# The work beside a recurrence gathered into one clump per slot

## The chip, the cores and the metric

The kernel runs on one core of one Trainium2 chip. The number that counts is the device time of one execution in microseconds; the kernel before takes 2278.77 us, the median of 3 runs (2270.02 to 2282.51). The core's engines run side by side, each through its own queue in order: PE (TensorE, with the weight load shown as PEld), DVE (VectorE), ACT (ScalarE), POOL (GpSimd) and SP, which issues the DMAs. They wait for each other through semaphores.

## The reference

Three layers follow each other. The first is a delta-rule recurrence over 768 tokens, for 4 batches of 8 heads of 48; the second a soft mixture of 8 experts over all 3072 tokens; the third a plain two-layer net.

```
for t in range(S):                                   # attention
    y[:, :, t] = einsum('bhd,bhde->bhe', q[:, :, t], state)
    v_old = einsum('bhde,bhd->bhe', state, kt)
    state = state + bt * einsum('bhd,bhe->bhde', kt, vt - v_old)
P = exp(logits - logits.max());  8 x (rows, then columns normalised)
out += P[:, e:e + 1] * (relu(x @ w1[e]) @ w2[e])     # for every expert e
h = x @ w_in;  h * sigmoid(1.702 h) @ w_out          # last layer
```

## The kernel before

The recurrence is done in 24 blocks of 64 tokens, one after the other (`u` = 0 to 23), each for two batches and all heads. `Attention.chain(u)` is the part that must be in order. It has four steps, `s` = 0 to 3, and each ends in one group of small fp32 matmuls and what frees them: `ks` (state times keys; DVE then makes `r`), `up` (the triangular inverse `tt` times `r`; ACT copies it to `su`), `sp` (the state's update; DVE makes `S`), `y` (the output; ACT makes `ys`). The stretch of the program that one step and all the work beside it take is a slot, and the slots are numbered 4u + s.

Beside the chain, three other kinds of work are put into the slots.

- `Attention.prep(g)` prepares the next group of four blocks; g counts the groups. It is a generator, and each `yield` is a piece. Its order is fixed: eight Gram pieces (`gram`, tile `pg`: 8 small matmuls, then three DVE products `am`, `x`, `x`), two ACT copies of `am`, a DVE transpose to `ln`, thirty steps of a triangular inverse on DVE alone (each an `lt` and an `ln` product, half a piece each), a transpose to `ta`, and then `pz`, `pz`, `px`, `px` (32 small matmuls each, copied by ACT) with DVE's transpose to `tt` and two ACT copies among them. How many pieces a slot gets is in `PIECES` (`FIRST` for the first 16 slots).
- `expert0(n)` is the first expert on the pair of blocks n, in full-array matmuls: `ph` (three matmuls of 256 columns per item; after three items ACT and DVE make the two halves of `h`) and `po` (three matmuls of 384 columns per item). One call of `expert_item` emits one item. Some five items fall on a slot (`ITEMS`, `RATE`), from slot 10 on.
- Once per block, at s = 1, `emit_x` turns the block before: PE transposes `ys` into `xt`, ACT and DVE split it into the two halves of `xb`, ACT copies it once more, and SP stores it. At even `u` the pair is then complete, its gates `pl` (9 matmuls on `xb`) come at s = 2, and their transpose `pt` at s = 3. The pair's `ph` read `xb` too.

The tiles `pg`, `pz`, `px`, `xt`, `pl` and `pt` share two PSUM buffers (pool `psg`): the third of them waits until the first has been read. `ph` has two buffers of its own. What the experts' items do not do beside the recurrence is done right after it by the same function; there is a fixed number of items in all (480).

In `slot` of the kernel before, the items are spread: a share before each piece and one after the last. `xt`, `pl` and `pt` are emitted ahead of the slot's pieces, and `xt` has at least one item in front of it.

Of the kernel before, what the change touches and what calls it, by code (L numbers as in the profile page):

```python
# [34 lines left out]
LAG = 10  # L35
# [5 lines left out]
class Attention:  # L41
# [127 lines left out]
    def gram(self, u, planes, h0, n, pool=None):  # L169


        nc, x, j, bm = self.nc, self.X[u // 2 % 4], u % 2, self.bm.get(u)
        hs = slice(h0, h0 + n)
        where, tag = pool or (self.psg, "g")
        ps = where.tile([128, n, len(planes), 64], F32, tag=tag, name="pg")
        for h in range(n):
            for b in range(2):
                dr = slice(64 * b, 64 * b + D)
                nc.tensor.matmul(  # L179
                    ps[64 * (1 - b):64 * (1 - b) + 64, h], x[dr, 0, j, h0 + h],  # L180
                    x[dr, planes[0] * (1 + b):planes[-1] * (1 + b) + 1:1 + b, j, h0 + h], start=True, stop=True)
        m = 8 * (u % 4) + h0
        if planes[0] == 0:
            nc.vector.tensor_tensor(out=self.am[:, m:m + n], in0=ps[:, :, 0], in1=bm[:, hs], op=ALU.mult)
        if planes[-1] == 1:
            for b in range(2):
                p = slice(64 * (1 - b), 64 * (1 - b) + 64)
                m = x[p, 1 + b, j, hs]
                if u < 4:
                    nc.scalar.copy(out=m, in_=ps[p, :, len(planes) - 1])  # L190
                else:
                    nc.vector.tensor_tensor(out=m, in0=ps[p, :, len(planes) - 1], in1=bm[p, hs], op=ALU.mult)
# [7 lines left out]
    def prep(self, g):  # L200

        nc, am, tt = self.nc, self.am, self.tt
        w, u = 2 * g, 4 * g
        if g == 0:
            self.square(0, nc.vector)
            self.square(1, nc.vector)
            self.norm(0)
            self.norm(1)
            self.weigh(0, 1)
            self.mask(0, eng=nc.vector)  # L210
            for v in range(1, 4):
                self.mask(v)
            for v in range(4):
                self.gram(v, (0,), 0, H, (self.psc, "c") if v < 2 else None)
            self.scale_v(0)
            self.scale_k(0)
            self.scale_k(1)
            self.square(2)
            yield 1.0
        else:  # L220
            for i in range(8):
                if i == 5:
                    self.mask(u + 3)
                self.gram(u + i // 2, (0, 1), i % 2 * 4, 4)
                if i == 1:
                    self.square(w + 1)
                elif i == 2:
                    self.norm(w + 1)
                elif i == 3:
                    self.weigh(w + 1)  # L230
                    self.mask(u + 2)
                elif i == 7:
                    self.scale_k(w)
                    self.scale_k(w + 1)
                yield 1.0

        ln = self.one.tile([128, 32, 32], F32, tag="ln", name="ln")

        for q in (32, 96):
            nc.scalar.copy(out=am[q:q + 32, :, 0:32], in_=am[q:q + 32, :, 32:64])  # L240
            yield 1.0
        nc.vector.transpose(out=ln, in_=am[:, :, 0:32].rearrange("p m t -> p t m"))
        yield 1.0
        nc.vector.memset(ln.rearrange("p t s -> p (t s)")[:, 0:1024:33], 1.0)
        for jj in range(1, 31):
            tmp = self.one.tile([128, 256], F32, tag="lt", name="lt")
            nr = 31 - jj
            t3 = tmp[:, 0:nr * jj].rearrange("p (a c) -> p a c", c=jj)
            nc.vector.tensor_tensor(  # L249
                out=t3, in0=ln[:, jj + 1:32, jj:jj + 1].to_broadcast([128, nr, jj]),  # L250
                in1=ln[:, jj:jj + 1, 0:jj].to_broadcast([128, nr, jj]), op=ALU.mult)
            yield 0.5
            nc.vector.tensor_tensor(out=ln[:, jj + 1:32, 0:jj], in0=ln[:, jj + 1:32, 0:jj], in1=t3, op=ALU.add)  # L253
            if g == 0 and jj < 5:
                self.gram(jj - 1, (1,), 0, H)

            if g < NG - 1:
                if jj == 17 and g > 0:
                    self.square(w + 2)
                elif jj == 21:  # L260
                    self.norm(w + 2)
                elif jj == 22:
                    step = self.weights(w + 2)
                elif jj > 22:
                    next(step, None)
            if jj == 30 and g < NG - 1:
                for v in range(2):
                    if g == 0:
                        self.mask_m(v)
                for v in range(2):  # L270
                    self.mask(u + 4 + v)
                    if g == 0:
                        self.mask_m(2 + v)
            yield 0.5
        ta = self.one.tile([128, 32, 32], F32, tag="ta", name="ta")
        nc.vector.transpose(out=ta.rearrange("p m s -> p s m"), in_=ln.rearrange("p t s -> p s t"))
        yield 1.0

        zs = ta

        def pz(m0, n):
            ps = self.psg.tile([128, n, 32], F32, tag="g", name="pz")
            for m in range(n):
                for q in (0, 64):
                    nc.tensor.matmul(ps[q + 32:q + 64, m], am[q:q + 32, m0 + m, 32:64],
                                     ta[q:q + 32, m0 + m], start=True, stop=True, tile_position=(q, q + 32))
            for q in (0, 64):
                nc.scalar.copy(out=zs[q + 32:q + 64, m0:m0 + n], in_=ps[q + 32:q + 64])

        def px(m0, n):  # L290
            ps = self.psg.tile([128, n, 32], F32, tag="g", name="px")
            for m in range(n):
                for q in (0, 64):
                    nc.tensor.matmul(ps[q:q + 32, m], zs[q + 32:q + 64, m0 + m],
                                     tt[q + 32:q + 64, m0 + m, 32:64], start=True, stop=True,
                                     tile_position=(q + 32, q))
            for q in (0, 64):
                nc.scalar.copy(out=tt[q:q + 32, m0:m0 + n, 32:64], in_=ps[q:q + 32])

        def tr(q):  # L300
            if q is None:
                nc.vector.transpose(out=tt[:, :, 32:64].rearrange("p m t -> p t m"), in_=ln)
            else:
                nc.scalar.copy(out=tt[q:q + 32, :, 0:32], in_=tt[q:q + 32, :, 32:64])

        for f, *i in (((pz, 0, 16), (tr, None), (pz, 16, 16), (tr, 0), (tr, 64), (px, 0, 16), (px, 16, 16)) if g else
                      ((pz, 0, 8), (tr, None), (tr, 0), (tr, 64), (px, 0, 8), (pz, 8, 8), (px, 8, 8),
                       (pz, 16, 16), (px, 16, 16))):
            while f == tr and self.upped < u - 1:
                yield 1.0  # L310
            f(*i)
            if f == px and i[0] == 0:
                self.ready = g
            yield 1.0
# [105 lines left out]
def kernel(  # L420
# [47 lines left out]
    A = Attention(tc, actx, ident, X, kq, kw, vw, bu, psg)  # L468
# [201 lines left out]
    ex = []  # L670
# [21 lines left out]
        while done < due and expert_item():  # L692
            done += 1

    def slot(t):

        n, k = rate * ITEMS[t % 16] if t >= LAG else 0, (PIECES if t > 15 else FIRST)[t % 16]
        if t == LAG:
            expert(BURST)
        i = 0  # L700
        while i < k:
            expert(n / (k + 1) * step[0])
            step[0] = next(prep, 1.0)
            i += step[0]
        expert(n / (k + 1))

    step = [1.0]
    build = sums(0, 0)
    for u in range(NU):
        for s, _ in enumerate(A.chain(u)):  # L710
            if s == 1 and u > 0:
                if 4 * u >= LAG:
                    due -= 1
                    expert(1)
                    done += expert_item()
                while u % 2 == 1 and len(ex) > 1:
                    done += expert_item()
                emit_x(u - 1, A.xt())
                if u % 2 == 0:
                    ex.append(expert0(u // 2 - 1))  # L720
            if s > 1 and u > 0 and u % 2 == 0:
                (logits if s == 2 else turn)(u // 2 - 1)
            slot(4 * u + s)
            while A.ready < u // 4:
                next(prep)
            next(ew, None)
            if u > 12:
                next(build, None)
# [418 lines left out]
```

## Time and profile before

| | |
|---|---|
| median of 3 runs | 2278.77 us (2270.02 to 2282.51) |
| the profiled execution | 2276.9 us, of which the span is 2275.2 us |
| PE busy in the span | 2169.0 us |
| DVE busy in the span | 1515.7 us |
| mean granted clock of TensorE, 1.00 being full | 0.982 |

In a row of the timeline, PE's shape is that of the stored weight (rows by columns), then that of the output. An fp32 matmul is recorded as two, so a Gram piece of 8 matmuls stands as x16 and a piece of `px` as x64. PE's durations contain the way through the array, so one matmul's end lies after the next one's start; what a matmul costs in a stream is the distance between starts. "L458" to "L460" are the three matmuls of `mm3`, which every full-array product is made of.

### The profile page before, as it was taken

What the parts mean: (1) busy time and instruction counts of PE and PEld (TensorE: products, weight loads), DVE (VectorE), ACT (ScalarE), POOL (GpSimd) and SP (SyncE); (2) the same over time, 40 slices, a digit from 0 to 9 for tenths busy, and PEclk for the clock granted to TensorE, in tenths of its full rate; (3) what the DMA queues carried; (4) which work ended last, traced back from release to release, by engine and by line L of the source; (5) the groups of instructions that cost most, each with busy time, mean ns of one, the idle gap of its engine ahead of it and who ended that gap; (6) DMA issues with size and microseconds to landing.
All of it is one profiled execution on the core that took longest, in us unless ns stands there. A gap on an engine that the chain in (4) does not pass through costs nothing.

```text
span 2275.2 us, 40538 instructions
## 1 busy us (share of the span) xinstructions
PE 2169.0 (95%) x15535; PEld 1950.2 (86%) x15535; DVE 1515.7 (67%) x2774; ACT 1057.4 (46%) x2117; POOL 1116.1 (49%) x1318
## 2 busy tenths in 40 slices
PE   3799899998999999999999999999999999999999
PEld 2788788897889989999989898888989998888988
DVE  7556755726667667766666777777775556676675
ACT  1434343443544444444445444444444446565554
POOL 4411131322767776666652556556565434672333
PEclk9799998999999999999999999999999999999999
DMA  4323333237343434333348565564554465567231
GB/s 106 99 57 89 91 87 108 83 102 284 133 155 132 170 127 146 122 140 124 125 156 293 174 183 171 172 210 162 194 187 146 139 239 164 160 184 246 92 118 49
DMA packets 229154, 336.73 MB, mean 148 GB/s; under 512 B 15648, under 2 KB 192416, under 8 KB 224800
## 3 DMA queue, kind: packets, MB, share of 16 engines
q1 hardware_dynamic: 228240, 333.26, 45.3%
q8 instruction: 122, 2.00, 0.4%
q10 hardware_dynamic: 720, 0.89, 0.1%
q14 instruction: 72, 0.59, 0.1%
HBM read 204.58 MB, written 129.50 MB: 147 GB/s over the span
## 4 chain that ended last, share of the span: by engine, by line
PE 72%; DVE 12%; POOL 6%; issue 3%; ACT 3%; DMA 2%; SPq 1%; POOLq 0%; ACTq 0%; DVEq 0%
PE po L458 12%; PE po L460 12%; PE po L459 12%; PE c L458 9%; PE c L459 9%; PE c L460 9%; DVE ln L253 3%; DVE lt L249 2%; PE pg L179 1%; PE ph L458 1%; POOL bv L528 1%; DMA w1r<-in_w_dram 1%; POOL w1c L455 1%; PE up L343 1%; PE ph L459 1%
## 5 line engine op out<-in xcount | busy, mean ns | idle before, releaser
L459 PE MATMUL po<-w2c,h 128*128 128x384 f32 x1728 | 587.5, 340 | 0.0
L460 PE MATMUL po<-w2c,h 128*128 128x384 f32 x1728 | 586.0, 339 | 0.9 <-DVE h L960 0.8
L458 PE MATMUL po<-w2c,h 128*128 128x384 f32 x1728 | 579.4, 335 | 0.8 <-ACT h L958 0.8
L1015 POOL TENSOR_TENSOR acc<-acc,ye 128x384 f32<-128x384 f32 x252 | 263.4, 1045 | 371.7 <-ACT ye L1014 361.5
L458 PE MATMUL c<-xt,w1c 128*128 128x512 f32 x1080 | 431.4, 399 | 13.7 <-DVE sg L957 5.8
L460 PE MATMUL c<-xt,w1c 128*128 128x512 f32 x1080 | 429.6, 398 | 2.6 <-POOL w1c L455 2.6
L459 PE MATMUL c<-xt,w1c 128*128 128x512 f32 x1080 | 428.5, 397 | 0.0
L992 DVE TENSOR_TENSOR o<-o,c 128x512 f32<-128x512 f32 x288 | 197.3, 685 | 255.7 <-PE c L460 232.5
L458 PEld LDWEIGHTS po<-w2c,h 128*128 128x128 f32 x1728 | 325.2, 188 | 40.6 <-ACT h L958 1.5
L1017 DVE SCALAR_TENSOR_TENSOR acc<-po,P,acc 128x384 f32<-128x384 f32 x420 | 258.3, 615 | 152.1 <-PE po L460 149.2
L459 PEld LDWEIGHTS po<-w2c,h 128*128 128x128 f32 x1728 | 324.1, 188 | 39.9
L460 PEld LDWEIGHTS po<-w2c,h 128*128 128x128 f32 x1728 | 325.3, 188 | 1.5 <-DVE h L960 1.5
L1014 ACT ACTIVATE ye<-po,P 128x384 f32<-128x384 f32 x252 | 146.3, 581 | 352.8 <-PE po L460 349.2
L460 PEld LDWEIGHTS c<-xt,w1c 128*128 128x128 f32 x1080 | 202.9, 188 | 48.0 <-POOL w1c L455 3.4
L458 PEld LDWEIGHTS c<-xt,w1c 128*128 128x128 f32 x1080 | 203.4, 188 | 45.7 <-DVE h L951 17.3
L459 PEld LDWEIGHTS c<-xt,w1c 128*128 128x128 f32 x1080 | 203.6, 188 | 8.9
L985 ACT COPY o<-c 128x512 f32<-128x512 f32 x288 | 163.8, 590 | 60.3 <-PE c L460 59.2
L949 ACT ACTIVATE h<-c 128x512 fp32r<-128x512 f32 x168 | 96.6, 598 | 176.4 <-DVE c L992 169.0
L1027 POOL TENSOR_TENSOR acc<-acc,ye 128x384 f32<-128x384 f32 x84 | 92.1, 1097 | 164.0 <-ACT ye L1026 158.0
L455 POOL TENSOR_TENSOR w2c<-w2r,w2c 128x384 fp32r<-128x384 f32 x140 | 146.4, 1046 | 45.6 <-ACT w2c L454 45.5
L992 DVE TENSOR_TENSOR f<-o,c 128x512 f32<-128x512 f32 x216 | 149.0, 690 | 12.4 <-PE c L460 3.3
L949 ACT ACTIVATE h<-f 128x512 fp32r<-128x512 f32 x168 | 100.1, 596 | 72.8 <-DVE f L992 70.7
(175 smaller groups left out, 3545.9 us busy)
## 6 DMA issues: line engine op xcount, KB each, us to landing
w1c<-wd SPq DMA_DIRECT2D x210, 384.0 KB, 4.5
wd<-w1c SPq DMA_DIRECT2D x28, 1920.0 KB, 7.0
xs<-bo SPq DMA_DIRECT2D x184, 128.0 KB, 2.2
xt<-xs SPq DMA_DIRECT2D x46, 512.0 KB, 6.0
w2r<-in_w_dram SPq DMA_DIRECT2D x55, 384.0 KB, 5.9
wd<-wo SPq DMA_DIRECT2D x56, 256.0 KB, 3.1
w1r<-in_w_dram SPq DMA_DIRECT2D x28, 384.0 KB, 7.7
x<-in_kq_dram SPq DMA_DIRECT2D x24, 384.0 KB, 6.3
```

The source lines that it names most:

```text
L253: nc.vector.tensor_tensor(out=ln[:, jj + 1:32, 0:jj], in0=ln[:, jj + 1:32, 0:jj], in1=t3, op=ALU.add)
L455: eng.tensor_tensor(out=dst_lo, in0=src, in1=dst_hi.bitcast(F32), op=ALU.subtract)
L458: nc.tensor.matmul(ps, lhs[0], rhs[0], start=start, stop=False, **kw)
L459: nc.tensor.matmul(ps, lhs[0], rhs[1], start=False, stop=False, **kw)
L460: nc.tensor.matmul(ps, lhs[1], rhs[0], start=False, stop=stop, **kw)
L949: nc.scalar.activation(out=h[:, 0], in_=src, func=ACTF.Relu)
L985: nc.scalar.copy(out=o, in_=ps)
L992: nc.vector.tensor_tensor(out=d, in0=o, in1=ps, op=ALU.add if how == "add" else ALU.subtract)
L1014: nc.scalar.mul(ye, ps, P[:, u, e:e + 1])
L1015: nc.gpsimd.tensor_tensor(out=a, in0=a, in1=ye, op=ALU.add)
L1017: nc.vector.scalar_tensor_tensor(out=a, in0=ps, scalar=P[:, u, e:e + 1], in1=a, op0=ALU.mult, op1=ALU.add)
L1027: nc.gpsimd.tensor_tensor(out=a, in0=a, in1=ye, op=ALU.add)
```

## The change

The slot's own pieces now follow the chain's step without anything between them, then comes what belongs to the turned tokens (`xt`, `pl` or `pt`, in the new function `turned`), then all the slot's items. If two pieces of a slot have used PE's small matmuls and more than one piece is left, half of the items are put there; `small` marks these pieces. The rule that put one item ahead of `xt` is gone. The numbers of pieces and items in a slot stay as they are.

```diff
@@ gram, pz and px, each at its start:
+        self.small = True
@@
-    def slot(t):
+    def slot(t, turned):
         n, k = rate * ITEMS[t % 16] if t >= LAG else 0, (PIECES if t > 15 else FIRST)[t % 16]
         if t == LAG:
             expert(BURST)
-        i = 0
+        i = m = 0
         while i < k:
-            expert(n / (k + 1) * step[0])
-            step[0] = next(prep, 1.0)
-            i += step[0]
-        expert(n / (k + 1))
-
-    step = [1.0]
+            A.small = False
+            i += next(prep, 1.0)
+            m += A.small
+            if m == 2 and i + 1 < k:
+                expert(n / 2)
+                n, m = n / 2, 0
+        turned()
+        expert(n)
+
+    def turned(u, s):
+        nonlocal done
+        if s == 1 and u > 0:
+            while u % 2 == 1 and len(ex) > 1:
+                done += expert_item()
+            emit_x(u - 1, A.xt())
+            if u % 2 == 0:
+                ex.append(expert0(u // 2 - 1))
+        if s > 1 and u > 0 and u % 2 == 0:
+            (logits if s == 2 else turn)(u // 2 - 1)
+
     build = sums(0, 0)
     for u in range(NU):
         for s, _ in enumerate(A.chain(u)):
-            if s == 1 and u > 0:
-                if 4 * u >= LAG:
-                    due -= 1
-                    expert(1)
-                    done += expert_item()
-                while u % 2 == 1 and len(ex) > 1:
-                    done += expert_item()
-                emit_x(u - 1, A.xt())
-                if u % 2 == 0:
-                    ex.append(expert0(u // 2 - 1))
-            if s > 1 and u > 0 and u % 2 == 0:
-                (logits if s == 2 else turn)(u // 2 - 1)
-            slot(4 * u + s)
+            slot(4 * u + s, lambda: turned(u, s))
```

On PE, the place after `up` of block u = 8, where the slot has two Gram pieces. `po` and `ph` are the expert's, `pg` a Gram piece. Before:

```order
L343 MATMUL up<-r,tt 64x48 x16
L458 MATMUL po<-w2s_200,h 128x384
L459 MATMUL po<-w2s_200,h 128x384
L460 MATMUL po<-w2s_200,h 128x384
L380 MATMUL xt<-ident,ys 128x128 x3
L179 MATMUL pg<-x_127 64x128 x8
L458 MATMUL po<-w2s_201,h 128x384
L459 MATMUL po<-w2s_201,h 128x384
L460 MATMUL po<-w2s_201,h 128x384
```

And now:

```order
L346 MATMUL up<-r,tt 64x48 x16
L180 MATMUL pg<-x_127 64x128 x16
L383 MATMUL xt<-ident,ys 128x128 x3
L461 MATMUL po<-w2s_201,h 128x384
L462 MATMUL po<-w2s_201,h 128x384
L463 MATMUL po<-w2s_201,h 128x384
L461 MATMUL po<-w2s_201,h 128x384
L462 MATMUL po<-w2s_201,h 128x384
L463 MATMUL po<-w2s_201,h 128x384
L461 MATMUL ph<-xb,w1s_186 128x256
```

Both Gram pieces (x16) now stand right behind `up`, and `xt` behind them, with the items after it.

On DVE, the slot of `up` of block u = 6, where the slot's pieces are four steps of the inverse. `xb` is the second half of the pair's split tokens, `h` the expert's, `S` the state made from the next slot's `sp`. Before:

```order
L455 TENSOR_TENSOR xb<-xt,xb 128x3x128
L249 TENSOR_TENSOR lt<-ln 128x234
L253 TENSOR_TENSOR ln<-ln,lt 128x18x13
L249 TENSOR_TENSOR lt<-ln 128x238
L253 TENSOR_TENSOR ln<-ln,lt 128x17x14
L249 TENSOR_TENSOR lt<-ln 128x240
L253 TENSOR_TENSOR ln<-ln,lt 128x16x15
L249 TENSOR_TENSOR lt<-ln 128x240
L253 TENSOR_TENSOR ln<-ln,lt 128x15x16
L607 SCALAR_TENSOR_TENSOR h<-ph,h 128x256
L360 TENSOR_TENSOR S<-S,sp 112x384
```

And now:

```order
L250 TENSOR_TENSOR lt<-ln 128x234
L254 TENSOR_TENSOR ln<-ln,lt 128x18x13
L250 TENSOR_TENSOR lt<-ln 128x238
L254 TENSOR_TENSOR ln<-ln,lt 128x17x14
L250 TENSOR_TENSOR lt<-ln 128x240
L254 TENSOR_TENSOR ln<-ln,lt 128x16x15
L250 TENSOR_TENSOR lt<-ln 128x240
L254 TENSOR_TENSOR ln<-ln,lt 128x15x16
L458 TENSOR_TENSOR xb<-xt,xb 128x3x128
L610 SCALAR_TENSOR_TENSOR h<-ph,h 128x256
L363 TENSOR_TENSOR S<-S,sp 112x384
```

`xb` stood ahead of the slot's eight products and now stands behind them.

## Rows read from the trace of the kernel before

**Rows 1.** Page, part 1: busy us, share of the span, instructions, by engine.
```profile
PE 2169.0 (95%) x15535; PEld 1950.2 (86%) x15535; DVE 1515.7 (67%) x2774; ACT 1057.4 (46%) x2117; POOL 1116.1 (49%) x1318
```

**Rows 2.** Engines by stretch: us, then busy time of PE, PEld, DVE, ACT, POOL; PEclk; DMA.
```profile
208.00:252.00 44.00, 44.00 (x713) 37.89 (x712) 19.92 (x48) 19.82 (x38) 7.81 (x6) 0.96 0.27 72
252.00:284.00 32.00, 26.57 (x350) 23.89 (x349) 29.37 (x87) 10.68 (x26) 3.34 (x3) 1.00 0.36 97
1000.00:1100.00 100.00, 100.00 (x507) 90.89 (x506) 68.76 (x113) 44.59 (x86) 62.43 (x69) 1.00 0.35 127
```

**Rows 3.** PE's waits, 83 to 506 us: waiter, releaser, us, times, longest.
```profile
PE pz L285 <- DVE ta L276: 10.2, 5, 2.5
PE ph L458 <- ACT xb L454: 1.2, 2, 1.0
```

**Rows 4.** Timeline, 225 to 228 us: start, us, engine, line, out<-in, [idle before].
```profile
225.40 0.34 PE L460 MATMUL po<-w2s,h 128*128 128x384 f32 x1
225.66 1.09 PE L179 MATMUL pg<-x 48*64 48x128 f32 x16
226.68 0.39 PE L458 MATMUL ph<-xb,w1s 128*128 128x256 f32 x1
226.91 0.28 PE L459 MATMUL ph<-xb,w1s 128*128 128x256 f32 x1
227.02 0.28 PE L460 MATMUL ph<-xb,w1s 128*128 128x256 f32 x1
227.24 0.86 DVE L192 TENSOR_TENSOR x<-pg,bm 64x256 f32<-64x256 f32 x2
```

**Rows 5.** Timeline, 217 to 219 us, the first piece of `px`.
```profile
217.13 0.34 PE L459 MATMUL po<-w2s,h 128*128 128x384 f32 x1
217.30 0.33 PE L460 MATMUL po<-w2s,h 128*128 128x384 f32 x1
217.56 1.20 PE L294 MATMUL px<-tt,ta 32*32 32x32 f32 x64
218.69 0.44 PE L458 MATMUL po<-w2s,h 128*128 128x384 f32 x1
218.97 0.33 PE L459 MATMUL po<-w2s,h 128*128 128x384 f32 x1
```

**Rows 6.** Groups by form, 83 to 540 us: busy us, mean ns, idle before.
```profile
L179 PE MATMUL pg<-x 48*64 48x128 f32 x536 | 38.0, 282 | 0.0
L294 PE MATMUL px<-tt,ta 32*32 32x32 f32 x640 | 12.2, 192 | 0.1
```

**Rows 7.** Timeline, 183 to 191 us, the pair's second tokens at u=6.
```profile
186.02 0.38 PE L458 MATMUL ph<-xb,w1s 128*128 128x256 f32 x1 [0.22 <-ACT xb L454]
186.06 0.55 DVE L455 TENSOR_TENSOR xb<-xt,xb 128x384 fp32r<-128x384 f32 x1
...
189.94 0.42 DVE L607 SCALAR_TENSOR_TENSOR h<-ph,h 128x256 fp32r<-128x256 f32 x1
190.27 0.55 DVE L360 TENSOR_TENSOR S<-S,sp 112x384 f32<-112x384 f32 x1
```

**Rows 8.** Timeline, 341 to 366 us, the same place at u=14 and after it.
```profile
341.81 0.29 PE L458 MATMUL pl<-xb,wgs 128*8 128x256 f32 x1
342.13 0.55 DVE L455 TENSOR_TENSOR xb<-xt,xb 128x384 fp32r<-128x384 f32 x1
...
353.22 0.58 PE L458 MATMUL ph<-xb,w1s 128*128 128x256 f32 x1 [2.61 <-DVE h L607]
365.63 1.72 PE L285 MATMUL pz<-ta,am 32*32 32x32 f32 x64 [1.73 <-DVE ta L276]
```

**Rows 9.** PE by stretch of 1 us: us, busy, PEclk, DMA share, GB/s.
```profile
283.00:284.00 1.00, 0.00 (x0) 1.00 0.73 188
285.00:286.00 1.00, 1.00 (x47) 0.50 0.05 16
290.00:291.00 1.00, 1.00 (x5) 0.57 0.37 82
```

More of the change, by code (lines that the diff above doesn't have):

```diff
@@ L281, in pz @@
         def pz(m0, n):
+            self.small = True
             ps = self.psg.tile([128, n, 32], F32, tag="g", name="pz")
@@ L290, in px @@
         def px(m0, n):
+            self.small = True
             ps = self.psg.tile([128, n, 32], F32, tag="g", name="px")
```

## The prediction

> **What bounds the kernel now.** I read the page's first part first. PE is busy for 95% of the span [rows 1], so an instruction elsewhere counts only where PE waits for it. The change touches only the stretch in which the recurrence runs, some 83 to 505 us, and the number of expert items done beside it stays the same; what is left over is done afterwards by PE alone. So a microsecond that PE saves or loses in this stretch moves the end by a microsecond, as long as PE is what the stretch waits for.
>
> Whether it is, I took from the engines by stretch. Each group of four blocks has two halves. From 208 to 252 us (the group's `pz`, `px` and the eight Gram pieces) PE is busy for all 44.00 us and DVE for 19.92: PE is the bound. From 252 to 284 us (the thirty steps of the inverse) DVE is busy for 29.37 of 32 us and PE for 26.57, so 5.4 us of PE are idle: DVE is the bound [rows 2]. PE's waits say the same: the largest is `pz` for DVE's transpose `ta`, 10.2 us in 5 times, which is the end of the DVE half [rows 3]. So the two halves must be priced apart: in the PE half each bubble counts, in the DVE half PE has some microseconds of cover, and what makes DVE later counts.
>
> **The change part by part.**
>
> *Fewer switches between small and full-array matmuls (PE half).* In PE's order before there are 137 stretches of small matmuls up to the last `y`, in the changed one 87. The 50 that vanish are 32 single Gram pieces and 18 single `pz` or `px`, which now adjoin a chain step or each other. What one costs alone: from the last full matmul at 225.40 to the second one behind the piece at 226.91 are 1.51 us; without the piece these two steps would be 0.17 (217.13 to 217.30) and 0.11 (226.91 to 227.02), so a Gram piece costs 1.23 us [rows 4, 5]. In the same way a `px` costs 218.97 - 217.30 - 2 x 0.17 = 1.33 us [rows 5]. What it costs in a stream: the 16 matmuls of the Gram piece stand as 1.09 us, the last one lasting 0.28, so 15 steps take 0.81 and 16 take 0.86; the 64 of `px` take (1.20 - 0.19) x 64/63 = 1.03 us [rows 4 to 6]. The whole saving is then 32 x 0.37 + 18 x 0.30 = 17 us. No row shows two pieces back to back at full speed, so I bound it: at the least only the two gaps at the edges go, 0.26 - 0.17 on entry and 0.23 - 0.11 on leaving [rows 4, 5], which is 50 x 0.2 = 10 us. I take 15, nearer to the upper end, since the rows of the piece itself give that one. A `y` or `sp` in front changes nothing in this.
>
> *PSUM waits (PE half).* `psg` has two buffers. `xt` now comes behind two Gram pieces and needs the first one's buffer. DVE is done with a piece 2.44 us after PE began it (225.66 to 227.24 + 0.86) [rows 4], two pieces take PE between 1.72 (streamed) and 2.0 us, so PE waits 0.4 to 0.7 us. The same holds for `pl` in the next slot, behind two more. That is at u = 4, 8, 12 and 16, eight waits of 0.6: 4.8 us. At u = 4 and 8 the pair's `ph` then wait for `xb`, which DVE makes behind the six products of the two pieces (at 2.44 + 3 x 0.43 = 3.7 us from the first one's start, 4.3 us when done): by the same count 0.2 and 0.45 us more than now, where `ph` waits 1.2 us in all for ACT's half [rows 3]. Together 5.5 us; ends 3 (half the waits covered because DVE is ahead) and 10 (`S`, 0.55 us [rows 7], in front each time).
>
> *`xb` behind the slot's products (DVE half).* In the slot after `up` DVE makes `xb` ahead of eight `lt`/`ln` products, and now behind them. At u = 6 it ended at 186.61, and the eight end at 189.94: 3.3 us later [rows 7]. The order at u = 6 has only one item of `po` between `xt` and the pair's first `ph`, which already waits now; its second matmul needs DVE's half and so starts 3.3 us later. Behind it on PE are the slot's `ph` and `sp`; for them waits DVE's `h` and then `S`, which stood at 190.27. From 189.9: nine `ph` at 0.11 to 0.12 make 191.0, `sp` 1.1, so `S` at 192.1, 1.8 us later on the engine that is the bound here, and up to 4 us if the clock has fallen in the wait. I take 3. At u = 14 nothing but `pl` waits: it did so already, 341.81 against an `xb` done at 342.68, and `xb` will be done at 346.0 [rows 8]. PE then idles 3.3 us longer, and the cover behind it is 2.61 us at 353.22 and 1.73 at `pz` [rows 8]: 0 to 1 us, I take 1. The like places at u = 10 and 18 I put between, 0.5 each. In the three last groups the `xb` of the slot with the last Gram piece also moves behind the transpose `ln`, into DVE's bound half: 3 x 0.55 = 1.7 us. Items after the slot's pieces leave DVE's `h` at the slot's end; the work ahead of each `r` and `S` is the same sum, so I cost that at nothing, and DVE's backlog hides it; without the backlog it would be one `h`, 0.42 us [rows 7], per slot. The longer waits bring one or two more falls of the clock, below: 2 us. Together 9 us, ends 2 (all covered) and 22 (four groups, 3.3 us and a fall each).
>
> *The clock.* At 283 us PE had nothing to do, and from 285 it ran at a granted clock of 0.50, the lower of its two levels (1.2 instead of 2.4 GHz), until it rose after 290 [rows 9]. So a fall lasts some 6 us here, and at half speed that costs up to 3 us of PE's work. Every group has one at its `pz` and will keep it: `pz` now lies right behind `sp`, PE arrives there one or two items earlier and waits longer for the same `ta`, but the last Gram piece lies as much earlier, so the sum is nothing.
>
> *Sum.* The profiled execution took 2276.9 us, 1.9 below the median of the runs (2278.77). 2276.9 - 15 + 5.5 + 9 = 2276.4, and against the median 2278.3. I predict 2276.5 us, between the two: no change that can be measured.
>
> In the page's row the share of PE's matmuls is full in the PE half, but PEld is busy for 37.89 of 44.00 us, 86%, against 91% at 1000 to 1100 us [rows 2]. The Trainium skill, page "Perfetto Trace Analysis", section "Identifying the Most-Contended Engine", says that matmul occupancy is a bad measure of headroom and that the weight loads' busy share is a good one. By that rule only the 5% between the two could be won: an estimate of 2.1 us for such a half, 9.5 us in four and a half groups instead of 15, and the sum would be 5.5 us higher. No run here shows yet which of the two is right.
>
> **The rivals.**
> *The clump wins in full.* The late `xb` falls into PE's idle 5.4 us of the DVE half in all groups [rows 2], and only the switches count: -17 + 3 + 2 gives -12, 2265 us. For it speaks that DVE is not delayed at u = 10, 14 and 18, where only `pl` waits; against it u = 6, where `h` and `S` hang on the late `ph`.
> *The late `xb` decides.* One mechanism: DVE's queue puts the pair's second half behind eight products, PE idles 3 to 4 us at u = 6, 10, 14 and 18, its clock falls there, and the chain's `sp` comes late, so that DVE, the bound, waits for PE as well. Price 22 against a switch saving at its lower end of 10 and waits of 5.5: +17, 2294 us. It decides from the point at which PE's wait for `xb` exceeds what it waits later in the same half (4.3 us at u = 14).
> *Small clumps pull the clock down in the PE half.* `y` and `pz` or `ks`, `px`, `px` are now 2 to 3 us without a full-array matmul. If each group lost one more fall of 3 us to this, +13, 2289 us. Against it: in the halves now the clock stays at 0.96 on average with the fall at `pz` already in it [rows 2].
>
> **How the numbers follow.** Forecast 0.45, full win 0.27, late `xb` 0.19, clock 0.09. About 0.5% of 2278.8, 11.4 us, is what a measurement of this kernel can tell from no change. The full win lies mostly beyond it, the two slow rivals mostly too, and the forecast inside except for a tenth: faster 0.28, same 0.44, slower 0.28. The likeliest case alone spans 2268 to 2285. The range that holds 8 in 10 must take in most of both sides: 2262 (the full win and 3 us) to 2294.
>
> **What would show it.** The order of PE between 208 and 252 us with fewer entries and steps of 0.05 us from one Gram piece to the next, and that half some 2 us shorter: the switches. PE's waits of about 0.6 us for DVE at `xt` and `pl`: the PSUM buffers. In the DVE half, waits of `ph` or `pl` for `xb` of 2 to 4 us, and a granted clock of 0.50 behind them; if they are there and the half is no longer than now, the cover held. I am wrong if the PE half is not shorter, or if the sum of the DVE halves grows by more than 10 us.

## The result, and the profile after

The change makes the kernel slower by about half a per cent.

| kernel | median of its runs (us) | beside it, the kernel before (us) | ratio, 95% interval |
|---|---|---|---|
| changed | 2291.24 (7 runs, 2286.84 to 2297.63) | 2275.89 | 1.0068, 1.0040 to 1.0095 |
| changed, second series | 2286.57 (6 runs, 2285.65 to 2289.53) | 2275.67 | 1.0052, 1.0035 to 1.0069 |

In microseconds that is 12 to 15. The forecast was 2276.5 and no change; the time lies inside the range of 2262 to 2294, but the forecast itself was wrong.

The profiled execution of the changed kernel took 2286.84 us with a span of 2285.1, so 9.9 more than the one before in either number. The page's first part says at once where to look. PE is *less* busy than in [rows 1], by 10.8 us, in a longer span:

```profile
PE 2158.2 (94%) x15535; PEld 1950.0 (85%) x15535; DVE 1520.2 (67%) x2774; ACT 1056.2 (46%) x2117; POOL 1117.2 (49%) x1318
```

The count of instructions and the busy time of the weight loads are unchanged (1950.2 before). So PE's work became shorter, and its idle time grew by about twice as much. The three stretches of [rows 2] in the changed kernel (us, then busy time of PE, PEld, DVE, ACT and POOL, granted clock, DMA):

```profile
208.00:252.00 44.00, 39.35 (x749) 36.42 (x746) 21.95 (x56) 17.22 (x35) 11.29 (x9) 0.96 0.29 74
252.00:284.00 32.00, 28.97 (x402) 25.70 (x400) 26.30 (x72) 12.57 (x28) 1.60 (x1) 1.00 0.40 100
1000.00:1100.00 100.00, 100.00 (x506) 90.84 (x505) 70.00 (x114) 46.16 (x87) 64.84 (x69) 1.00 0.33 122
```

The group's halves have shifted by some 10 us against these bounds, so they are no measure of a half. They do show that PE no longer fills a Gram stretch (39.35 of 44 us instead of all of it). What it waits for there stands in PE's list of waits, 83 to 506 us (waiter, releaser, us, times, longest), which answers to [rows 3]:

```profile
PE pz L287 <- DVE ta L277: 15.0, 5, 4.0
PE up L346 <- DVE r L337: 6.6, 4, 2.5
PE pl L462 <- DVE xb L458: 6.1, 3, 2.3
PE ph L462 <- DVE xb L458: 5.7, 3, 4.2
PE ph L461 <- DVE h L610: 3.8, 4, 2.0
PE po L463 <- DVE h L610: 2.9, 3, 1.5
PE px L297 <- issue: 2.7, 4, 0.9
PE xt L383 <- DVE x L193: 2.5, 4, 0.7
PE pl L461 <- DVE x L193: 2.5, 4, 0.7
```

Before, `pz` waited 10.2 us, `pl` and `ph` 1.1 us for DVE's half of `xb`, `ph` and `po` 4.3 us for `h`, and `up` 9.0 us for `r`; the `px`, `xt` and `pl <- x` lines did not exist. New are therefore 10.7 us for `xb`, 5.0 us for the two PSUM buffers, 4.8 at `pz`, 2.7 at `px` and 2.4 for `h`, less 2.4 at `up`: 23.2 us.

**An account of PE's time.** From stretches of 1 us I added up two things: the idle share of each (1 minus PE's busy time) and the time lost to the clock (busy time times 1 minus the granted clock). What is left of a difference in span is then PE's work at full clock. From 83 to 520 us the idle time grows from 27.1 to 50.2 us, by 23.1, which agrees with the list above. Over 83 to 620 us, which takes in the falls of the clock just behind the recurrence:

| kernel | span against before | idle | lost to the clock | PE's work at full clock |
|---|---|---|---|---|
| before | 0 | 40.6 | 32.4 | 0 |
| changed | +9.9 | 62.7 | 38.0 | -17.8 |
| changed, second profile | +8.9 | 58.1 | 41.2 | -17.4 |

The last column is the span's difference less the growth of the two before it, for the changed kernel 9.9 - 22.1 - 5.6. So the change does what its name says and wins 17 to 18 us of PE's work, and then loses 26 to 28 to waits and to the clock.

**The saving.** Two Gram pieces now stream into each other and into the chain step ahead, PE's timeline from 238 us (start, us, engine, line, out<-in):

```profile
238.56 0.28 PE L180 MATMUL pg<-x 48*64 48x128 f32 x1
238.60 0.22 PE L357 MATMUL sp<-su,bk 64*64 64x48 f32 x1
238.66 1.92 PE L180 MATMUL pg<-x 48*64 48x128 f32 x31
```

The first `pg` starts before the last matmul of `sp`, and 30 further steps take 1.92 - 0.28 = 1.64 us, 0.055 each. Before, one piece of 16 cost 1.23 us with its edges [rows 4].

**The late `xb` at u = 6.** The place of [rows 7], in the changed kernel, shortened; of the slot's eight products only the first (on an `lt` of 234) and the last are shown:

```profile
186.97 0.55 PE L383 MATMUL xt<-ident,ys 128*128 128x128 f32 x3
...
187.95 0.47 ACT L457 CAST xb<-xt 128x384 fp32r<-128x384 f32 x1
...
188.47 0.39 PE L461 MATMUL ph<-xb,w1s 128*128 128x256 f32 x1 [0.42 <-ACT xb L457]
...
189.09 0.40 DVE L250 TENSOR_TENSOR lt<-ln 128x234 f32<-128x234 f32 x1
...
192.17 0.41 DVE L254 TENSOR_TENSOR ln<-ln,lt 128x240 f32<-128x240 f32 x1
192.50 0.55 DVE L458 TENSOR_TENSOR xb<-xt,xb 128x384 fp32r<-128x384 f32 x1
193.08 0.48 ACT L503 COPY x<-xt 128x384 f32<-128x384 f32 x1 [4.66 <-DVE xb L458]
...
193.10 0.58 PE L462 MATMUL ph<-xb,w1s 128*128 128x256 f32 x1 [4.24 <-DVE xb L458]
...
195.11 1.94 PE L357 MATMUL sp<-su,bk 64*64 64x48 f32 x32
...
197.10 0.55 DVE L363 TENSOR_TENSOR S<-S,sp 112x384 f32<-112x384 f32 x1 [0.98 <-PE sp L357]
```

ACT's half of `xb` is there at 188.42. DVE's half comes behind the slot's products at 192.50, so PE's second `ph` stands 4.24 us. It goes on at half speed: `sp` takes 1.94 us instead of 1.13, and DVE, the bound of this half, waits 0.98 us for it. PE in stretches of 2 us (us, busy, granted clock):

```profile
188.00:190.00 2.00, 0.44 (x2) 1.00 0.00 0
190.00:192.00 2.00, 0.00 (x0) 1.00 0.00 0
192.00:194.00 2.00, 0.90 (x4) 0.55 0.00 0
194.00:196.00 2.00, 2.00 (x25) 0.50 0.39 107
```

The same wait stands at u = 10, 14 (the place of [rows 8]) and 18, at `pl`, which before waited once, 0.64 us; in the second profile these are 0.28, 2.15 and 0.86 us:

```profile
276.03 0.29 PE L462 MATMUL pl<-xb,wgs 128*8 128x256 f32 x1 [1.63 <-DVE xb L458]
...
355.99 0.38 PE L462 MATMUL pl<-xb,wgs 128*8 128x256 f32 x1 [2.15 <-DVE xb L458]
...
442.73 0.28 PE L462 MATMUL pl<-xb,wgs 128*8 128x256 f32 x1 [2.31 <-DVE xb L458]
```

To follow the chain I compared the starts of `up` in both profiles. The changed kernel lags by 2.8 us at u = 6, 10.3 at u = 8, 7.9 at u = 10, 10.6 at u = 12, 9.8 at u = 14, 15.6 at u = 16 and 15.1 at u = 20. It gains up to 2.4 us in a Gram half (u = 8 to 10) and loses up to 7.5 in the stretch of an inverse with the `pz` and `px` at its end (u = 6 to 8).

### The profile page after: what moved, and what is told of

The parts are those of the page before. It is cut to its first block, busy times and chain, and to the rows that moved or that the text cites. A ratio compares the mean times of both kernels' runs of the same rounds, so it can differ in the third digit from the quotient of the medians.

```text
span 2285.1 us, 40543 instructions
## 1 busy us (share of the span) xinstructions
PE 2158.2 (94%) x15535; PEld 1950.0 (85%) x15535; DVE 1520.2 (67%) x2774; ACT 1056.2 (46%) x2117; POOL 1117.2 (49%) x1318
## 4 chain that ended last, share of the span: by engine, by line
PE 76%; DVE 12%; POOL 5%; issue 2%; ACT 2%; DMA 2%; SPq 0%; POOLq 0%; ACTq 0%; DVEq 0%
PE po L463 13%; PE po L462 12%; PE po L461 12%; PE c L461 10%; PE c L462 9%; PE c L463 9%; DVE lt L250 3%; DVE ln L254 2%; PE ph L461 1%; PE ph L462 1%; PE ph L463 1%; PE pg L180 1%; DMA w1r<-in_w_dram 1%; POOL w1c L458 1%; POOL bv L531 1%
```

## The experiments

Each ran beside the kernel before on the same chip; all but e4 have 10 to 12 runs. There were four groups, each on a chip of its own: e1, e3, e4, e5; e2, e6, e7, e8; e9, e10, e12 and the changed kernel's second series; e13, e14, e15. Across groups I compare the ratios. "First" and "last" say where the turned tokens, logits and gates (`turned()`) stand against the slot's own pieces. Ratios are to the kernel before.

| kernel | turned work in Gram slots | in the inverse's slots | items | median (us) | ratio, 95% interval |
|---|---|---|---|---|---|
| e1 | first | first | clumps | 2283.21 | 1.0032, 1.0017 to 1.0046 |
| e3 | last | first | clumps | 2278.24 | 1.0010, 0.9995 to 1.0025 |
| e4 (7 runs) | first | last | clumps | 2288.51 | 1.0052, 1.0033 to 1.0072 |
| e5 | as changed, copy first | | clumps | 2282.54 | 1.0026, 1.0015 to 1.0038 |
| e2 | last | last | spread | 2284.34 | 1.0044, 1.0026 to 1.0062 |
| e6 | last | first | clumps in Gram blocks only | 2278.00 | 1.0006, 0.9991 to 1.0021 |
| e7 | as e6, copy first | | as e6 | 2276.93 | 1.0011, 0.9999 to 1.0023 |
| e8 | as before, copy first | | spread | 2283.78 | 1.0042, 1.0028 to 1.0056 |
| e9 | last | first | clumps in five Gram slots only | 2269.53 | 0.9976, 0.9962 to 0.9990 |
| e10 | behind half of the items | first | as e9 | 2265.70 | 0.9960, 0.9947 to 0.9973 |
| e12 | as before | as before | spread, clump in the `px` slot | 2281.73 | 1.0027, 1.0013 to 1.0041 |
| e13 | last | last | clumps, spread at `pz` and `px` | 2280.12 | 1.0026, 1.0011 to 1.0041 |
| e14 | as e10 | first | as e10, clumps in the inverse | 2263.69 | 0.9954, 0.9937 to 0.9970 |
| e15 | as e10 | last | as e10 | 2274.64 | 0.9994, 0.9977 to 1.0011 |

### Where the turned work stands: e1, e3, e4

The theory was that the late `xb` costs nearly all; the rivals were the clumps themselves, and the PSUM waits. The edit of e3, cut at ` ...` (e1 calls `turned()` first always, e4 has `< 2`):

```
+        first = t // 4 % 4 > 1
+        if first:
+            turned()
         while i < k:
 ...
-        turned()
+        if not first:
+            turned()
         expert(n)
```

> The changed kernel, but the turned tokens, the logits and the turned gates stand ahead of the slot's own pieces in every slot, as before the change; the expert items stay in their clumps. Theory (late xb): between the chain's steps the changed kernel loses some 2.8 + 7 + 0 + 7 + 4.8 = 21.6 us at u = 2, 6, 10, 14 and 18, where the second half of xb stands behind eight products, and 5 us in eight waits for a PSUM buffer at xt and pl; both go, so 2291 - 27 = about 2265 us (2260 to 2271), and no wait of ph or pl for xb above 1.2 us. Rival (the clumps themselves): the losses come from expert items that lie at the slot's end, whose h then delays S; only the 5 us of PSUM waits go: about 2286 us.

> The changed kernel, but turned tokens, logits and gates stand ahead of the slot's pieces only in the blocks whose slots hold the steps of the inverse (u mod 4 = 2 or 3); behind the Gram pieces they stay last. Theory (late xb): the 21.6 us go and the 5 us of PSUM waits stay: about 2270 us (2265 to 2276). Rival (clumps themselves): 2291, within 4 us. Rival (PSUM waits of xt and pl start it all): 2291 as well, since these waits stay.

> The other half alone: ahead of the slot's pieces only in the blocks with Gram pieces (u mod 4 = 0 or 1), last in the slots of the inverse. Theory (late xb): only the eight PSUM waits of 0.6 us go: about 2286 us (2282 to 2290), and the waits for xb at u = 6, 14 and 18 are still there with 2 to 4 us each. Rival (PSUM waits start it all, the late xb being covered): about 2270 us.

e3 gives back 10 to 13 us of the changed kernel's loss, less than the 21.6 that the theory read from the lag, and e4 nothing that can be told from the changed kernel. e1 is 5 us slower than e3. In Gram slots the turned work last is thus right: with `xt` in front, `pg` no longer adjoins `up`, and by the account e1 wins 12.2 us of PE's work where e3 wins 16.9. What e3 still waits for, 83 to 506 us:

```profile
PE pz L287 <- DVE ta L277: 16.5, 5, 4.8
PE ph L461 <- DVE h L610: 8.9, 7, 3.9
```

The waits for `xb` are gone (0.9 us are left), those for `h` and at `pz` have grown. So the lag had lumped two causes together, and the next question was what the clumps cost.

### ScalarE's copy: e5, e7, e8

In the changed kernel ScalarE's float32 copy `x` of the turned tokens waits 47.2 us in 22 times for DVE's `xb` (19.2 in 24 times before), with `h` behind it in ScalarE's queue. The edit puts the copy ahead of DVE's half (the tiles' names are shortened here):

```
-        split(hi, lo, xt)
-        keep(0, u, xt, x32)()
+        nc.scalar.copy(out=hi, in_=xt)
+        keep(0, u, xt, x32)()
+        nc.vector.tensor_tensor(out=lo, in0=xt, in1=hi, op=ALU.subtract)
```

> The changed kernel, but ScalarE's float32 copy of the turned tokens is written ahead of VectorE's half of xb, so that it no longer waits for VectorE; the order of PE and VectorE is the changed kernel's. At u = 18 this copy waited 4.8 us for xb with the relu half of h queued behind it on ScalarE. Theory (PE's wait for xb is what costs): PE's waits for xb stay, 2 to 5 us are won at the places where h stood behind the copy: about 2288 us (2284 to 2292). Rival (ScalarE's queue decides): h comes on time at u = 6, 10, 14 and 18, S with it, and 10 us or more are won: 2280 us or less.

> e6_spread_in_inverse with ScalarE's float32 copy of the turned tokens ahead of VectorE's half of xb. In the changed kernel this edit gave 8 us back. Theory (the copy matters where xb is late): early xb in the slots of the inverse leaves it little to do, 0 to 4 us less than e6: about 2263 us. Rival (the copy holds ScalarE's queue wherever it stands): 6 to 8 us less than e6, 2257 us.

> The kernel before with ScalarE's float32 copy of the turned tokens ahead of VectorE's half of xb, nothing else. There this copy waits 19.2 us in 24 times for xb, 3.1 at the most, against 47.2 us in the changed kernel. Theory (it matters only where xb is late): 2275 us, within 4. Rival (the copy holds ScalarE's queue wherever it stands): about 8 us faster, 2267 us.

In the changed kernel it gives 6 to 10 us back, between the two expectations; on e6 nothing that can be told; and on the kernel before it *costs* 9.6 us, which neither theory had. In the account the span of e8 is 7.3 us longer, of which idle time is 1.3 and the clock 6.1. The profile shows where one fall of the clock lies. DVE's `xb` now waits for the copy, which takes 0.48 us. At u = 4 that lengthens one wait of PE from 0.21 us to this:

```profile
148.92 0.39 PE L459 MATMUL ph<-xb,w1s 128*128 128x256 f32 x1 [0.58 <-DVE xb L515]
```

and PE's stretches of 2 us show what follows (the kernel before holds 1.00 in all stretches from 142 to 162 us):

```profile
148.00:150.00 2.00, 1.42 (x12) 1.00 0.24 65
150.00:152.00 2.00, 2.00 (x21) 0.59 1.04 316
152.00:154.00 2.00, 2.00 (x18) 0.50 0.98 290
154.00:156.00 2.00, 2.00 (x18) 0.50 0.09 25
```

The rate of 0.50 lasts to 160 us, and the lag grows from 2.5 us at `up` to 7.4 at `y` of u = 4. That the wait, longer by 0.37 us, caused the fall is not shown. In the changed kernel the waits at this place are the same in its two profiles (0.57 and 0.21 us, 0.57 and 0.20); in the first the clock falls behind them, at 151 us, in the second it stays at 1.00. And e5 has the longer second wait too, 0.59 us, with the clock at 1.00 behind it. So a single execution can't say what one short wait costs, and why e8 loses 9.6 us stays open but for the account. Which waits e5 shortened I can't settle either: its profiled execution, 2287.85 us, lies 5 above its own median. What the runs do show is that a gain of 6 to 10 us by such an edit in one order says nothing about another.

### The late work alone: e2

The kernel before with the turned work moved behind the slot's pieces, items spread as ever:

```
             i += step[0]
+        turned()
         expert(n / (k + 1))
```

(and the call in the loop over `s` taken out).

> The kernel before with one edit: the turned tokens, logits and gates are called behind the slot's own pieces; the expert items stay spread between the pieces. Theory (the late xb costs by itself): with turned work late in all slots the changed kernel was 13 us slower than with it early in the slots of the inverse, so here some 10 to 15 us over the kernel before: about 2287 us, and waits of ph or pl for xb of 2 to 4 us. Rival (late xb costs only where items lie in a clump behind it, since spread items are work for PE while xb comes): within 4 us of before, 2275 us.

It costs 10 us (0.44%, 0.26 to 0.62), the lower end of what the theory said, and the waits for `xb` are like those of the changed kernel; at u = 6 (and 1.63 us at u = 10):

```profile
187.75 0.58 PE L459 MATMUL ph<-xb,w1s 128*128 128x256 f32 x1 [4.14 <-DVE xb L455]
```

In the account its span is 10.4 us longer, idle time 8.5 and the clock 1.8: the work itself is unchanged to 0.2 us, as it should be where no switch is moved. For e8, which moves none either, the remainder is 0.1 us.

### Clumps in the inverse, and at px: e6, e9, e12

e6 is e3 with the items spread in the inverse's slots; e9 spreads them in every slot but the five with Gram pieces, by one condition (cut at ` ...`):

```
-        if t // 4 % 4 > 1:
+        if not 1 <= t % 16 <= 5:
             turned()
             while i < k:
                 expert(n / (k + 1) * step[0])
 ...
```

e12 is the kernel before with `expert(0 ...)` between the pieces of the one slot `t % 16 == 0`, and all its items behind them.

> As e3_first_in_inverse, and in the slots of the inverse (u mod 4 = 2 or 3) the expert items are spread between the pieces as before the change; in the Gram blocks they stay in clumps with the turned work last. In the profile of e3 the Gram halves gained about 13.5 us over the kernel before and the inverse halves lost about 15, where PE's waits for VectorE's h rose from 4.3 to 12.3 us and the one of pz for ta from 10.2 to 16.5. Theory (clumped items wait for their own h, and PE comes to pz with nothing left): the 15 go, about 2265 us (2260 to 2270), with PE's waits for h at 4 to 6 us. Rival (the two halves only shift the same work, what Gram blocks win the inverse must lose): 2278 us, as e3.

> As e6_spread_in_inverse, and the items are spread in every slot but the five with Gram pieces (t mod 16 = 1 to 5), so also between ks, px and px. In the profile of e6 PE waits 6.7 us in 3 places at px, right behind ks, while ScalarE still copies tt (2.11 us), and the clock falls behind it (216 to 223 us); in the kernel before nine ph and three po lie between. Theory (px has lost its cover): these waits go, with a fall or two of the clock: e6 less 7 to 12 us, about 2268 us (2264 to 2272). Rival (what PE gains in the Gram blocks it waits for in the inverse, whatever stands where): 2278 us as e3 and e6.

> The kernel before with one slot in sixteen changed (t mod 16 = 0): there the two px follow ks at once and the slot's items come behind them. Theory (px waits for ScalarE's copies of tt, and the clock falls): some 2.5 us of wait in three or four groups and a fall of 3 us each, less about 5 us for switches: 2283 us (2279 to 2288). Rival (the wait is covered, only switches count): 2271 to 2275 us.

e6 reads as e3: my theory that clumped items in the inverse wait too long for their own `h` fell. But its profile had a line that I had not counted, `px`, at 212 to 219 us:

```profile
211.94 1.14 PE L335 MATMUL ks<-S,x 48*64 48x48 f32 x32
...
213.01 1.38 PE L297 MATMUL px<-tt,ta 32*32 32x32 f32 x75
...
213.59 2.11 ACT L307 COPY tt<-tt 32x1024 f32<-32x1024 f32 x2
...
216.85 1.65 PE L297 MATMUL px<-tt,ta 32*32 32x32 f32 x53 [2.46 <-issue]
```

The second of two adjoining `px` stops in its middle: the row at 213.01 holds the 64 matmuls of the first `px` and 11 of the second, and the other 53 begin 2.46 us after it. The expectations of e9 and e12 took this for a wait for ScalarE's copies of `tt`, 2.11 us long. The times refute that: the first `px` and part of the second ran before or while these copies ran, the row names no releaser ("issue"), and in the kernel before `px` starts at 217.56 [rows 5] while the same two copies run (216.35 to 218.46). What does lie beside the stop is a transfer of PE's own instructions. From 213.6 to 215.4 us the DMA view has

```profile
q8 instruction: 1, 0.02, 5.9%
```

one packet of 16,384 bytes, under way from 213.66 to 215.36 in the trace; PE goes on 1.50 us after its end. This queue brings 122 such packets in the whole kernel, one for some 255 of PE's matmuls and weight loads. All 36 stops of `px` under "issue" of 0.2 us or more, in fourteen of the profiles, are alike: PE goes on 1.26 to 1.85 us after such a packet has ended. And from kernel to kernel they stand at the same places of PE's own stream (behind 1494 matmuls at u = 4, 2637 to 2639 at u = 8, 3780 to 3783 at u = 12, 4923 to 4927 at u = 16), whatever work lies around them; from one to the next are some 1143 matmuls and as many weight loads, and nine packets.

So PE runs out of instructions there: the 107 matmuls from `ks` to the stop, and as many weight loads, are gone through in 2.45 us (211.94 to 214.39), before the next packet is in. No run changes the packets, so this cause is read from the traces and not tested by an edit. In the kernel before, nine `ph` and three `po` lie between `ks` and `px`; a `ph` holds PE for 0.11 us or more, a matmul of `px` for 0.016 [rows 4, 5], and no such stop is in PE's list of waits.

Behind the stop of e6 the stretches say:

```profile
214.00:216.00 2.00, 0.39 (x25) 1.00 0.01 2
216.00:218.00 2.00, 1.15 (x44) 0.59 0.03 8
```

With items put between (e9) `px` waits 1.4 us instead of 6.7, 7 us come back, and the kernel is faster than before, as expected to the microsecond or two. The reverse, e12, adds the stops to the kernel before and costs 6 us:

```profile
PE px L294 <- issue: 7.7, 4, 2.6
```

### An item ahead of xt: e10

```
+        expert(n / 2)
         turned()
-        expert(n)
+        expert(n / 2)
```

> As e9_spread_px_too, but in the five Gram slots half of the slot's items lie between the Gram pieces and the turned work and half behind it. Theory (waits for the PSUM buffer, 8 of 0.63 us in the profiles of the changed kernel, e3 and e6 alike): two or three items, 0.7 to 1 us of PE, cover them: 5 us less than e9, about 2263 us. Rival (those waits are given back by the next wait for DVE): as e9.

The waits of `xt` and `pl` for the PSUM buffer fall from 5.0 us to 0.6, and 3.8 us are won between the medians. The two intervals overlap, and the profiled executions have it the other way (2270.70 us against 2268.70), so the size is rough; the waits are gone for certain.

### How it splits in the changed kernel itself: e13, e14, e15

> The changed kernel once more, unchanged, so that it stands on one chip with the others and its size is known better than from seven runs (1.0068, 1.0040 to 1.0095). All theories: 2285 to 2293 us, 10 to 16 us above the kernel before.

The second series, in the first table, makes the changed kernel 2286.57 us. e13 is the changed kernel with the items spread in the three slots that hold `pz` and `px` alone:

```
+        if t % 16 in (14, 15, 0):
+            while i < k:
+                expert(n / (k + 1) * step[0])
+                step[0] = next(prep, 1.0)
+                i += step[0]
+            turned()
+            expert(n / (k + 1))
+            return
```

e14 is e10 with `expert(0)` between the pieces of `t % 16 = 6` to 13 and all items behind them. e15 is e10 with `turned()` behind the pieces instead of ahead of them, in all slots but the five.

> The changed kernel, but in the three slots in sixteen that hold pz and px (t mod 16 = 14, 15, 0) the items are spread as before the change; turned work last everywhere, items clumped elsewhere. The changed kernel stands at about 2288 us (13 runs on two chips). Theory (px without cover costs a wait and a fall of the clock in each group, as e9 against e6 with 8 us): 2280 us (2277 to 2284). Rival (in the changed kernel px waits only 2.5 us in all, since other waits come first): 2286 to 2289 us.

> As e10_item_before_xt, but in the eight slots of the inverse's steps (t mod 16 = 6 to 13) the items stand in a clump behind the steps; turned work stays first there. Theory (clumped items wait for their own h: PE's waits for h were 12.3 us in e3 against 6.2 in e6): 4 to 8 us more than e10, about 2272 us. Rival (DVE's half has room for it, as e3 and e6 with 2278 each say): 2266 us, as e10.

> As e10_item_before_xt, but in the slots of the inverse (all but t mod 16 = 1 to 5) the turned work stands behind the slot's pieces, the items being spread. Theory (the late xb costs by itself, as e2 against before with 9 us): 2275 us (2272 to 2279), with waits for xb of 2 to 4 us at u = 6, 14 or 18. Rival (it costs only together with clumped items): 2266 us.

e13 wins 0.26 to 0.42% of the changed kernel, 6 to 10 us, though by the account it wins only 11.3 us of PE's work where the change wins 17 to 18. The gain lies where the edit is: from the end of the transpose `ta` to that of the next `ln`, four stretches that hold `pz`, `px` and the Gram pieces, e13 is 14.1 us shorter than the kernel before and the changed kernel 5.9 and 5.8 in its two profiles; from `ln` to `ta`, the five DVE halves, they are longer by 24.1 and by 23.8 and 20.0. Its waits, 83 to 506 us, keep those for `xb` and lose those at `px` (none is left) and over a third of those at `pz`:

```profile
PE pz L287 <- DVE ta L277: 9.2, 5, 2.5
...
PE ph L462 <- DVE xb L458: 5.7, 3, 4.2
...
PE pl L462 <- DVE xb L458: 3.0, 3, 1.9
```

e14 equals e10: clumps in the inverse cost nothing that can be told, as e3 and e6 had said. Its lines, 83 to 506 us, show why I had misread e3: the waits for `h` are there, with `pz` back at 9.0. One stop at `px` is left in it:

```profile
PE pz L287 <- DVE ta L277: 9.0, 5, 2.3
...
PE ph L461 <- DVE h L610: 7.0, 7, 2.3
PE px L297 <- issue: 3.1, 1, 3.1
```

e15 loses 0.34% against e10, 7.7 us (0.40% against e14, on the same chip): the late `xb` costs by itself, with everything else in order. At 0.9954 and 0.9960, e14 and e10 are faster than the kernel before by 9 to 10.5 us, and than the changed one by more: Gram pieces in clumps, turned work last only behind them and with items ahead of it, and items between `pz`, `px` and the chain.

## Why the prediction was wrong

**The step that failed** is the count of 18 single `pz` and `px` among the 50 switches that vanish, at a gain of 18 x 0.30 = 5.4 us, with the sentence that PE "arrives there one or two items earlier and waits longer for the same `ta`, but the last Gram piece lies as much earlier, so the sum is nothing". In the changed kernel `pz` waits 15.0 us instead of 10.2 and `px` 2.7 instead of none, and to have their items back is worth 6 to 10 us (e13; 7 in e6 to e9, 6 in e12). So this term is not -5 but +6 to +10, 11 to 15 us off, which is the size of the miss. I had priced the switch around these pieces, and not that the items taken out of it were cover: `pz` waits for DVE's `ta`, and `px` for PE's own instructions, which clumped small matmuls use up faster than they come. No row was read for `px` but its duration. The prediction's own sign of being wrong came true as well: measured from `ln` to `ta`, the DVE halves grew by 20 to 24 us in all, more than the 10 that it allowed. Some 10 us of that are also in e10 and e14 (9.9 and 10.6), and may only be items that now stand behind `ln` and not ahead of it; the rest goes with the late `xb` and whatever the causes add to each other.

**The switches** were right: 17 us in full and 15 taken, 17.4 to 17.8 measured by the account. The stretches of small matmuls are 137 before and 87 in the changed kernel, as the prediction counted; e12 has 128 and wins 4.1 us of work. By the rule of the Trainium skill (page "Perfetto Trace Analysis", section "Identifying the Most-Contended Engine") only an estimate of 9.5 us of headroom was left. The trace disagrees: the busy time of the weight loads is the same to 0.2 us in both kernels, and 17 us of PE's work were won.

**The PSUM waits** were right: eight of 0.63 us, 5.0 in all, against eight of 0.6 and 4.8. Taking them away is worth about 3.8 us (e9 to e10).

**The late `xb`** was sized at 9 us, and by itself costs 7.7 (e15 against e10) to 10 (e2). Its parts were wrong: PE waits 1.2 us at u = 2, where I had nothing, 4.2 at u = 6, where I had 3.3 more than the 0.3 of before, and 2.2 and 0.9 to 2.3 at u = 14 and 18, where I had counted on the cover of later waits. What I took for one or two falls of the clock, 2 us, is 5.6 and 8.8 us in the two profiles, over all causes.

**Items at the slot's end at nothing** was right (e14, e6).

**The rivals.** "The late `xb` decides" came nearest with 2294 us and names a real cost, but not all: with it alone e2 stands at 2284 and e15 at the kernel before. "The clump wins in full" names the time that e10 and e14 reach, -9 to -10.5 us, but not their way: 105 stretches of small matmuls are left in them, so 32 of the 50 switches are gone, and by the account they win 9.6 and 8.8 us of PE's work, not 17. (e9 has 105 as well and shows 15.0; why is open.) That small clumps pull the clock down in the PE half is not borne out: e3 keeps the clumps at `pz` and `px`, its clock is 1.00 from 209 to 283 us, and the clock costs it 23.2 us in 83 to 520 us against 27.3 before.

**What stays open.** From e14 (-10.5 us) one adds 7.7 for the late `xb`, 3.8 for the PSUM waits and 6 to 10 for `pz` and `px` and gets +7 to +11; measured are +12 and +15 in the two series. The intervals of the terms, 3 to 5 us each, cover the rest, and no run tells whether the causes also strengthen each other. How e5 wins its 6 to 10 us is open as well.

## What to carry to other kernels

When independent work is gathered into a clump, price two things for each place that it leaves: the switch that is saved, and the wait that this work was covering. The second has two parts here. One is found by asking of each instruction that now stands first what its operands wait for (`pz`). The other isn't in the operands: small matmuls behind each other can use up PE's instructions (`px`), and a stop without a releaser, at the same count of PE's instructions in every kernel, is the sign of it. Work that another engine makes (here DVE's half of a pair) belongs ahead of that engine's long queue, and its consumer behind a clump, not in front of it. And count idle time and clock apart: the remainder tells whether the work itself got shorter, even when the total got longer.

## What the runs showed of the hardware

- PE stops in a dense run of small matmuls until 1.26 to 1.85 us after a packet of 16,384 bytes of instructions has landed: 36 times for 0.2 to 3.1 us in the profiles here, always near the same counts of its own matmuls. This is read from the traces; no run changed the packets. In or behind each such stop of e6 and e12, 1.2 us and more, the granted clock fell to 0.50; behind those of e3, 0.8 us at the most, it stayed at 1.00.
- The clock does not follow the length of a short wait alone: behind the same waits of 0.57 and 0.2 us it fell to 0.50 in one profile of the changed kernel (at 151 us) and stayed at 1.00 in the other.
- The account of idle time and granted clock closes to 0.2 us in the two kernels that move no switch (e2, e8), though single executions of one kernel differ by 10 us. So the remainder can be trusted to some tenths there; where switches move, e9's 15.0 against e10's 9.6 us shows that it is rougher.
- ScalarE's copy of the turned tokens waits for DVE's `xb`, though it reads only `xt`, as long as it is written behind it (47.2 us in 22 times); written ahead of it, the wait is gone from ScalarE's list and DVE waits instead.
